# Half of a conformer's first pointwise product by seven products at the turn of groups, its weight sums kept in a buffer of x

## The chip, the cores and the metric

The kernel runs on one core of a Trainium2 chip. The metric is the device time of one launch in microseconds (us), the median of several runs. Of the five engines that run side by side, TensorE (PE) multiplies matrices into eight PSUM banks of 128 x 512 fp32; VectorE (DVE) and ScalarE (ACT) read these banks and work on SBUF; GpSimd (POOL) does small things; SyncE (SP) issues nearly all DMAs, in order. An engine runs its instructions in the order of the program and waits at semaphores.

## The reference, cut to what matters

A conformer block on x of 2 x 4000 x 512 in bf16: a feed-forward layer, attention over the 4000 tokens of a batch, a convolution module, a second feed-forward layer, with layer norms between. The change is about the start of the convolution module:

```
h = _layernorm(x2, axis=-1)
h = h @ w_pw1
a = h[..., :D].copy()
b = h[..., D:].copy()
h = a * _sigmoid(b)
```

D is 512, so w_pw1 has 512 rows and 1024 columns: "the first pointwise product". A depthwise convolution with three taps over the tokens follows.

## The kernel before, in words

Tokens go in 16 chunks of 512, 8 a batch; the last of each batch has 416 (`width`). Three stages follow each other: the first feed-forward layer over all chunks, the attention in 16 groups (one per chunk of queries, loop `attention`, L2050), and the second feed-forward layer. What is between attention and the second layer for chunk t (output projection, layer norm, pointwise product, gate, taps) is done beside the attention of the groups t + 1 and t + 2.

A group g runs through 32 steps kt. In the first group of a batch (g = 0 and 8, "plain") each step multiplies one tile of 128 keys with the queries (`scores`). In the others, steps 2 to 29 are taken four at a time by a quad (`score_quad`, L1993): a 2 x 2 block product of four key tiles is made from seven products instead of eight (Strassen's scheme in Winograd's form). Product k takes sums of key blocks times sums of query blocks; partial results are added in three PSUM banks (0, 1, 2, called c, x, h) and one SBUF buffer, m5. Its chain is: products 5 and 1, copied by ACT to m5 and h; product 6 added into h, then DVE writes x = h + m5; product 7 added into h, DVE writes m5 = h + m5; product 4 added into h. Products 2 and 3 go on top of c and x. ACT takes the exponentials. The values are multiplied in the same way (`pv`), products 2 and 4 of group g only in steps 2 to 6 of group g + 1 (`late_third`, L2133). The turn of groups, steps 30, 31, 0 and 1, has no quads.

The pointwise product (`pw1`, L2405) is made plainly before: for each of eight blocks of 128 channels four matmuls of 128 x 128 by 512 tokens, PSUM to `conv_b` (L2361: blocks of b, tanh of half of it by ACT) or `conv_a` (L2372: blocks of a, and the gate (tanh + 1) * a by DVE). `pair` (L2733) puts a block of b and one of a together and, two ticks on, the taps of the chunk before (`taps_beside`). Pairs 0 and 1 of chunk t stand at steps 24 and 28 of group t + 1, pairs 2 and 3 at steps 3 and 5 of group t + 2.

x of a chunk is fetched from DRAM for the residual (`get_x`, L2751, step 22) and stored again (`put_x`, L2754), in slots 0 and 1 of the buffer `xt` by turns during the attention. `touch` (L968) fills the unused 96 columns of bank 1 by a matmul for chunks of 416.

The order within each engine is not that of the program text. `Plan` (L110) collects all operations with modelled durations and simulates the engines; `choose` (L289) picks for PE, among the blocks ready within 8 us of modelled work behind the oldest open one, the one that can start first, and of equal ones the earlier in the text. All instructions are so emitted by L93.

Of the kernel before, what the change touches and what calls it, by code (L numbers as in the profile page):

```python
# [5 lines left out]
F32 = mybir.dt.float32  # L6
# [11 lines left out]
CHUNK = TPC * TILE  # L18
# [86 lines left out]
class Node:  # L105

    __slots__ = ("e", "emit", "dur", "land", "preds", "succs", "left", "ready", "late", "at", "seq", "ev", "size", "turn", "other")


class Plan:  # L110
# [7 lines left out]
    def __init__(self, sync, ahead, beside):  # L118
        self.S, self.ahead, self.beside = sync, ahead, beside
        self.nodes, self.pe, self.block = [], [], []  # L120
        self.w, self.r, self.d = {}, {}, {}
        self.table, self.same, self.first = None, [], None

    @staticmethod
# [48 lines left out]
    def new(self, e, dur, land, emit, reads, writes, dkeys=()):  # L173
        n = Node()
        n.e, n.dur, n.land, n.emit, n.preds, n.succs, n.seq, n.at = e, dur, land, emit, set(), [], len(self.nodes), len(self.pe)
        n.size, n.turn, n.other = 0, False, None
        self.nodes.append(n)
        n.preds |= self.link(n, reads, writes, dkeys)
        return n
# [92 lines left out]
    def once(self):  # L272
# [16 lines left out]
        def choose(e):  # L289
            if e == "PE":  # L290
                best = None
                for n in wait["PE"]:
                    k = index[n]
                    if T[k] - T[head] > self.beside:
                        continue
                    key = (max(free[e], n.ready - (40 if k == head else 0)), k)
                    if best is None or key < best[0]:
                        best = (key, n)
                return best and (max(free[e], best[1].ready), best[1])
            limit = T[head] + self.ahead  # L300
            found = [n for n in wait[e] if T[n.at] <= limit]
            if not found:
                return None
            now = max(free[e], min(n.ready for n in found))
            can = sorted([n for n in found if n.ready <= now], key=lambda n: (n.late, n.seq))
            soon = [n for n in found if n.ready > now]
            for n in can:
                end = now + max(n.other[e][0] if n.other else n.dur, n.size / 260) + self.OVER[e]
                if all(end <= u.ready + 60 or u.late >= end or u.late >= n.late for u in soon):
                    return now, n  # L310
            u = min(soon, key=lambda n: n.ready)
            return max(free[e], u.ready), u
# [37 lines left out]
class Sync:  # L350
# [125 lines left out]
    def emit_dma(self, engs, dkey, fns, reads, writes):  # L476
# [14 lines left out]
        self._bind(ev, reads, writes)  # L491
        return ev

    def planned(self, ahead, beside):
# [56 lines left out]
class Conformer:  # L551
# [35 lines left out]
    def memory(self):  # L587
# [114 lines left out]
        self.b_QF = [X.buf("QF", o, 4 * HC) for o in homes]  # L702
        self.m5s, self.b_m5s = X.view(18432 + 12 * HC, CHUNK, F32), X.buf("m5s", 18432 + 12 * HC, 4 * CHUNK)
        self.hv = A.view(TCB * 4096, 2 * PAIRS * D).rearrange("p (n k e d) -> p n k e d", k=2, e=2, d=HD)
        self.hq = A.view(2048, QUADS * 2048).rearrange("p (q u r e j k) -> p q u r e j k", q=QUADS, u=2, r=2, e=2, j=2)
# [152 lines left out]
        self.b_m3 = [C.buf("m3", oP + (self.NP - 1) * 1024 + j * 2 * TILE, 2 * TILE) for j in range(TPC)]  # L858

        self.last7, self.b_last7 = C.view(oLT + 4096, CHUNK), C.buf("last7", oLT + 4096, 2 * CHUNK)  # L860
        self.hl = C.view(oHL, 1024).rearrange("p (h c k) -> p h c k", h=2, c=DC)
# [102 lines left out]
    def mm(self, out, lhsT, rhs, start, stop, reads, bank, inc=None, **kw):  # L964
        self.S.op("PE", lambda e: e.matmul(out, lhsT, rhs, start=start, stop=stop, **kw),
                  reads=reads, writes=[bank], inc=stop if inc is None else inc)

    def touch(self, ps, b_ps, W):  # L968
        if W < CHUNK and b_ps is self.bank(1)[1]:
            x = self.hT[0][:, 0, 0, :]  # L970
            self.mm(ps[:, W:CHUNK], x, x[:, 0:CHUNK - W], False, True, [self.b_hT[0][0]], b_ps, skip_group_check=True)

# [664 lines left out]
    def q_group(self, b, qc, dc):  # L1637

        s, sl = qc % 2, self.query_slot(b, qc)
        ps, b_ps = self.sbank()  # L1640
        W = width(qc)
        lin, lo = self.queries(qc, sl)
        for cc in range(DC):
            self.mm(ps[:, 0:W], self.M[:, cc, dc * 128:(dc + 1) * 128], lin[:, cc, lo:lo + W],
                    cc == 0, cc == DC - 1, [self.b_M] + self.b_lnT[sl], b_ps)
        self.touch(ps, b_ps, W)
        self.act(self.qT[s][:, dc, 0:W], ps[:, 0:W], AF.Copy, [b_ps], [self.b_qT[s][dc]])
# [345 lines left out]
    def score_quad(self, g, q, step):  # L1993
# [34 lines left out]
        if step == 0:  # L2028
            product(5, h, b_h, True)
            self.act(m5, h[:, 0:W], AF.Copy, [b_h], [b_m5])  # L2030
            product(1, c, b_c, True)
# [18 lines left out]
    def attention(self, old, hook):  # L2050

        for g in range(NCK):
            W, plain = width(g), g % TCB == 0
            for kt in range(KT):
# [4 lines left out]
                if plain and kt < KT - 1 or kt < 2 or kt == KT - 2:  # L2059
                    ps, b_ps = self.scores(g, kt, None if plain else self.bank((0, 2)[kt] if kt < 2 else 0))  # L2060
                    if kt < KT - 2:
                        self.exp_pair(g, kt, ps, b_ps)
                    else:
                        self.act(self.P30[:, 0:W], ps[:, 0:W], AF.Exp, [b_ps], [self.b_P30], scale=SCALE)
                elif not plain and kt < KT - 2:
                    self.score_quad(g, *divmod(kt - 2, 4))
                if g == 0 and kt < 2:
                    self.pop(old // 2 if kt == 0 else old - old // 2)
# [8 lines left out]
                self.keys_swap(g, kt)  # L2077
                self.tick()

    @staticmethod  # L2080
# [324 lines left out]
    def pw1(self, t, cb, bank=None):  # L2405
# [9 lines left out]
        for out, x in moves:  # L2415
            for cc in range(DC):
                self.mm(out, self.Wp1[:, cc, cb * 128:(cb + 1) * 128], x[:, cc], cc == 0 and out is moves[0][0], cc == DC - 1,
                        [self.b_Wp1] + self.b_lnT[1 if t == NCK - 1 else 0], b_ps, skip_group_check=True)
        if t < NCK - 1:
            self.touch(ps, b_ps, W)  # L2420
        return ps, b_ps
# [46 lines left out]
    def fetch_conv(self, t):  # L2468
        W = width(t)
        self.load(self.dcv4[t][:, :, 0:W], self.dcvd[t].rearrange("p (c k) -> p c k", c=DC)[:, :, 0:W], self.b_dcv[t],  # L2470
                  reads=self.b_dcvd[t])

    def halo_left(self, t, jj):
# [155 lines left out]
    def program(self, any_score):  # L2629
# [100 lines left out]

        tail = NCK - 2

# [8 lines left out]
        def att_hook(g, kt):  # L2741
            if g == 0 and kt == 8:
                self.load(self.Wp1, i["w_pw1"].rearrange("(c p) f -> p c f", p=128), [self.b_Wp1])
            if kt in here and (0 <= g - 1 < tail or g - 1 == tail and here.index(kt) < self.KEEP):
                pair(g - 1, here.index(kt), self.bank(1) if kt == 24 else None)
            if 0 <= g - 2 < tail and kt in there:
                pair(g - 2, 2 + there.index(kt))
            if g == 0 and self.rest:
                self.load_rest(FC + kt, 3)
            if kt == (12 if any_score else 22):  # L2750
                self.get_x(g, self.slot(g, 0, 2))  # L2751
            if g and kt == 9 and not any_score:
# [14 lines left out]

        last = NCK - 1
        if any_score:
# [257 lines left out]
```

## Time and profile before

| | |
|---|---|
| median of three runs | 1884.49 us (1883.29 to 1886.34) |
| the profiled execution | 1882.47 us |
| its span, first to last instruction | 1878.7 us |
| DVE busy | 1463.0 us |
| ACT busy | 1306.9 us |
| TensorE clock granted | 1.0 of full speed |

In the profile a row gives line, engine, operation, what is written and read by the program's names (`s` are the banks 0 to 3, `y` the banks 4 to 7, `work`, `wff`, `keys`, `sums` and `xt` are SBUF regions), shapes, count, then busy us, mean ns of one, and the idle time before with its releaser. In the timeline a row is start, duration, engine, operation. PE's matmuls overlap, so that the duration of one holds the latency of its end.

### The profile page before, as it was taken

To read this page: it belongs to the slowest core of one execution; us is meant where nothing else is said; L and a number is where in the kernel's file an instruction comes from. 1 tells how busy PE (TensorE), PEld (TensorE's weight loads), DVE (VectorE), ACT (ScalarE), POOL (GpSimd) and SP (SyncE) were. 2 spreads that over 40 slices of the span, in tenths; PEclk is the share of its full clock that TensorE was granted. 3 is DMA by queue.
4 is the path that set the end of the run, shared out by engine and by line. 5 is a ranking of instruction groups with operands and counts; after the bars stand their busy time and mean duration, and the time that the engine had idled before them with its cause. 6 is when DMAs were issued, how large, how long until landed. Compare 5 with 4: busy or idle time off the path is not lost.

```text
span 1878.7 us, 39230 instructions
## 1 busy us (share of the span) xinstructions
PE 1860.1 (99%) x15389; PEld 1442.7 (77%) x15389; DVE 1463.0 (78%) x3191; ACT 1306.9 (70%) x2419; POOL 133.2 (7%) x301
## 2 busy tenths in 40 slices
PE   9999999999999999999999999999998999999998
PEld 5888888866777777777677777777774888888886
DVE  7888888868667777776777677768778888888885
ACT  5777777644667777677667677777668687777773
POOL 1000000000000000000000000000011000000000
PEclk9999999999999999999999999999999999999999
DMA  7323344197545555447944444444375222222111
GB/s 191 101 79 91 80 113 105 57 265 214 173 144 151 158 170 166 107 133 177 248 125 133 130 122 114 122 137 121 111 203 171 74 61 71 77 46 61 49 43 33
DMA packets 325014, 231.52 MB, mean 123 GB/s; under 512 B 204179, under 2 KB 295638, under 8 KB 324566
## 3 DMA queue, kind: packets, MB, share of 16 engines
q1 hardware_dynamic: 324294, 228.68, 44.4%
q8 instruction: 123, 2.02, 0.4%
q14 instruction: 69, 0.57, 0.1%
q10 hardware_dynamic: 528, 0.26, 0.0%
HBM read 128.44 MB, written 55.79 MB: 98 GB/s over the span
## 4 chain that ended last, share of the span: by engine, by line
PE 97%; DVE 1%; ACT 1%; DMA 0%; issue 0%; DVEq 0%; ACTq 0%
PE s L93 48%; PE y L93 48%; DVE work L93 1%; ACT work L93 0%; DMA xt<-v12d 0%; DVE wff L93 0%; DVE xt L93 0%; DVE s L93 0%; ACT sums L93 0%; DMA work<-work 0%; ACT wff L93 0%; ACT keys L93 0%; ACT s L93 0%; ACT xt L93 0%; ACT L93 0%
## 5 line engine op out<-in xcount | busy, mean ns | idle before, releaser
L93 ACT ACTIVATE sums<-s 128x512 bf16<-128x512 f32 (+2 forms) x494 | 288.2, 584 | 171.3 <-PE s L93 169.9
L93 ACT ACTIVATE keys<-s 128x512 bf16<-128x512 f32 (+2 forms) x284 | 165.6, 588 | 183.6 <-PE s L93 166.4
L93 DVE TENSOR_TENSOR sums<-sums 128x512 bf16<-128x512 bf16 (+3 forms) x528 | 195.4, 398 | 75.0 <-ACT sums L93 70.0
L93 PE MATMUL y<-work,keys 128*128 128x256 bf16 x1920 | 244.6, 273 | 0.0
L93 PE MATMUL s<-work,keys 128*128 128x256 bf16 (+5 forms) x1456 | 224.5, 292 | 0.0
L93 ACT ACTIVATE work<-xt,work 128x512 bf16<-128x512 bf16 x268 | 206.7, 785 | 7.8 <-DVE work L93 7.8
L93 PE MATMUL y<-wff,keys 128*128 128x256 bf16 (+3 forms) x1592 | 209.1, 276 | 0.1
L93 PEld LDWEIGHTS y<-work,keys 128*128 128x128 bf16 x1920 | 187.8, 98 | 25.1
L93 PE MATMUL y<-sums,keys 128*128 128x256 bf16 (+1 forms) x1440 | 202.6, 270 | 0.0
L93 PE MATMUL s<-sums 128*128 128x256 bf16 x1296 | 193.8, 273 | 0.0
L93 DVE TENSOR_TENSOR keys<-keys 128x1024 bf16<-128x1024 bf16 (+2 forms) x262 | 169.2, 662 | 28.8 <-ACT keys L93 13.6
L93 PE MATMUL y<-work,wff 128*128 128x256 bf16 (+2 forms) x1116 | 184.0, 292 | 0.0
L93 PEld LDWEIGHTS y<-wff,keys 128*128 128x128 bf16 (+1 forms) x1592 | 151.2, 98 | 32.4 <-issue 3.3
L93 DVE BATCH_NORM_STATS2 work<-xt 128x6 f32<-128x512 bf16 x251 | 163.9, 680 | 5.1 <-DMA xt<-in_x_dram 4.3
L93 PEld LDWEIGHTS s<-work,keys 128*128 128x128 bf16 (+1 forms) x1456 | 119.2, 97 | 50.6 <-ACT sums L93 4.0
L93 PEld LDWEIGHTS y<-sums,keys 128*128 128x128 bf16 x1440 | 138.8, 98 | 24.1 <-DVE sums L93 0.6
L93 POOL TENSOR_TENSOR work<-work 128x4 f32<-128x4 f32 (+3 forms) x107 | 89.8, 840 | 807.4 <-DVE work L93 804.9
L93 PE MATMUL s<-work,wff 128*128 128x512 bf16 (+5 forms) x668 | 141.0, 345 | 3.2 <-DVE work L93 2.7
L93 PEld LDWEIGHTS s<-sums 128*128 128x128 bf16 x1296 | 126.7, 98 | 20.0
L93 PE MATMUL s<-work 128*128 128x512 bf16 (+4 forms) x565 | 138.5, 375 | 3.0 <-DVE work L93 1.8
L93 PE MATMUL y<-sums,xt 128*128 128x256 bf16 (+1 forms) x960 | 139.4, 270 | 1.5 <-DVE sums L93 0.8
L93 PEld LDWEIGHTS y<-work,wff 128*128 128x128 bf16 x1116 | 108.2, 98 | 29.8
(143 smaller groups left out, 3202.2 us busy)
## 6 DMA issues: line engine op xcount, KB each, us to landing
xt<-kfd SPq DMA_DIRECT2D x98, 384.0 KB, 3.3
xt<-v12d SPq DMA_DIRECT2D x105, 256.0 KB, 2.9
xd<-xt SPq DMA_DIRECT2D x28, 512.0 KB, 3.1
xt<-xd SPq DMA_DIRECT2D x28, 512.0 KB, 4.3
out_dram<-xt SPq DMA_DIRECT2D x14, 512.0 KB, 3.0
xt<-in_x_dram SPq DMA_DIRECT2D x13, 512.0 KB, 4.0
dcvd<-wff SPq DMA_DIRECT2D x48, 128.0 KB, 2.1
keys<-dcvd SPq DMA_DIRECT2D x12, 512.0 KB, 4.3
```

The costliest lines, as they stand in the source:

```text
L93: return getattr(eng, self.name)(*self.args, **self.kw)
```

## The change

For chunks 0 to 6 and 8 to 13 (`by_unit`) pairs 0 and 1 are replaced by a unit of seven products (`gate_unit`) in four parts: at steps 30 and 31 of group t + 1 and 0 and 1 of group t + 2; where group t + 2 is plain, the last three all at step 31. It uses banks 0, 1, 2 and the m5 buffer of the quads. Its left blocks are channels of a and b (256 each) by halves of the 512 rows; its right ones are halves of the rows by halves of the tokens. Each product is four matmuls of 256 columns. The weights' sums (`gate_weights`) are made once, in group 0, into slot 1 of `xt`; the tokens' differences (`gate_tokens`) for each chunk at steps 26 to 29, into the buffer that the layer norm used. The pairs at steps 24 and 28 are then pairs 2 and 3. x of a chunk is fetched at step 26 and always into slot 0, of the last chunk into slot 1.

Besides: product 5 of a quad goes to bank x instead of h; the single scores of steps 0 and 1 both go to bank 0 (1 used bank 2 before); `touch` goes; and the planner's rule for equal blocks of PE compares modelled start times, in which the quads are put 1000 ns ahead (`front`).

```diff
@@ -120 +120 @@
+        self.front = 0
@@ -173 +174 @@
         n.e, n.dur, n.land, n.emit, n.preds, n.succs, n.seq, n.at = e, dur, land, emit, set(), [], len(self.nodes), len(self.pe)
-        n.size, n.turn, n.other = 0, False, None
+        n.size, n.turn, n.other, n.front = 0, False, None, self.front
@@ -293 +294 @@
-                    key = (max(free[e], n.ready - (40 if k == head else 0)), k)
+                    key = (max(free[e], n.ready - (40 if k == head else 0)), T[k] - n.front)
                     if best is None or key < best[0]:
@@ -491 +492 @@
+    def front(self, ns):
+        if self.plan:
+            self.plan.front = ns
     def planned(self, ahead, beside):
@@ -701 +706 @@
         self.m5s, self.b_m5s = X.view(18432 + 12 * HC, CHUNK, F32), X.buf("m5s", 18432 + 12 * HC, 4 * CHUNK)
+        self.WS = X.view(4096, 2048).rearrange("p (m j d) -> p m j d", m=4, j=2)
+        self.b_WS = [X.buf("WS", 4096 + m * 1024, 1024) for m in range(4)]
@@ -857 +864 @@
+        self.TF = [C.view(oLM + m * 1024, 512).rearrange("p (t j k) -> p t j k", t=2, j=2) for m in range(4)]
+        self.b_TF = [C.buf("TF", oLM + m * 1024, 1024) for m in range(4)]
+        self.th2 = W.view(24576, 2 * CHUNK, F32).rearrange("p (u k) -> p u k", u=2)
@@ -964 +974 @@
-    def touch(self, ps, b_ps, W):
-        if W < CHUNK and b_ps is self.bank(1)[1]:
-            x = self.hT[0][:, 0, 0, :]
-            self.mm(ps[:, W:CHUNK], x, x[:, 0:CHUNK - W], False, True, [self.b_hT[0][0]], b_ps, skip_group_check=True)
@@ -1643 +1648 @@
                     cc == 0, cc == DC - 1, [self.b_M] + self.b_lnT[sl], b_ps)
-        self.touch(ps, b_ps, W)
         self.act(self.qT[s][:, dc, 0:W], ps[:, 0:W], AF.Copy, [b_ps], [self.b_qT[s][dc]])
@@ -2026 +2030 @@
         if step == 0:
-            product(5, h, b_h, True)
-            self.act(m5, h[:, 0:W], AF.Copy, [b_h], [b_m5])
+            product(5, x, b_x, True)
+            self.act(m5, x[:, 0:W], AF.Copy, [b_x], [b_m5])
             product(1, c, b_c, True)
@@ -2049 +2053 @@
+        S = self.S
         for g in range(NCK):
@@ -2057 +2062 @@
                 if plain and kt < KT - 1 or kt < 2 or kt == KT - 2:
-                    ps, b_ps = self.scores(g, kt, None if plain else self.bank((0, 2)[kt] if kt < 2 else 0))
+                    ps, b_ps = self.scores(g, kt, None if plain else self.bank(0))
                     if kt < KT - 2:
...
                 elif not plain and kt < KT - 2:
+                    S.front(1000)
                     self.score_quad(g, *divmod(kt - 2, 4))
+                    S.front(0)
+                self.unit_steps(g, kt)
                 if g == 0 and kt < 2:
@@ -2076 +2084 @@
                 self.tick()
+    UNIT = (30, 31, 32, 33)
+    def unit_steps(self, g, kt):
+        if g == 0 and 24 <= kt < 28:
+            self.gate_weights(kt - 24)
+        for t, at in ((g - 1, kt), (g - 2, kt + KT)):
+            if self.by_unit(t):
+                if 26 <= at < 30:
+                    self.gate_tokens(at - 26)
+                for n, k in enumerate(self.UNIT):
+                    if min(k, KT - 1) == at if (t + 2) % TCB == 0 else k == at:
+                        self.gate_unit(t, n)
@@ -2416 +2438 @@
-        if t < NCK - 1:
-            self.touch(ps, b_ps, W)
         return ps, b_ps
@@ -2469 +2489 @@
+    @staticmethod
+    def by_unit(t):
+        return 0 <= t < NCK - 2 and t % TCB != TCB - 1
+    def gate_weights(self, step):
+        S = self.S
+        a11, a12, a21, a22 = [self.Wp1[:, 2 * e:2 * e + 2, lo:lo + 256] for lo in (D, 0) for e in range(2)]
+        s1, s2, s4, s3 = [self.WS[:, m] for m in range(4)]
+        b1, b2, b4, b3 = [[b] for b in self.b_WS]
+        out, x, y, op, rd, wr = ((s1, a21, a22, ALU.add, [], b1), (s2, s1, a11, ALU.subtract, b1, b2),
+                                 (s4, a12, s2, ALU.subtract, b2, b4), (s3, a11, a21, ALU.subtract, [], b3))[step]
+        S.op("DVE", lambda e: e.tensor_tensor(out=out, in0=x, in1=y, op=op), reads=rd + [self.b_Wp1], writes=wr)
+    def gate_tokens(self, step):
+        q = lambda e, k: self.lnT[0][:, 2 * k:2 * k + 2, 2 * e:2 * e + 2, :]
+        t1, t2, t4, t3 = self.TF
+        b1, b2, b4, b3 = [[b] for b in self.b_TF]
+        out, x, y, rd, wr = ((t1, q(0, 1), q(0, 0), [], b1), (t2, q(1, 1), t1, b1, b2), (t3, q(1, 1), q(0, 1), [], b3),
+                             (t4, q(1, 0), t2, b2, b4))[step]
+        self.S.op("DVE", lambda e: e.tensor_tensor(out=out, in0=x, in1=y, op=ALU.subtract),
+                  reads=rd + self.b_lnT[0], writes=wr)
+    def gate_unit(self, t, step):
+        S = self.S
+        (c, b_c), (x, b_x), (h, b_h) = [(ps[:, 0:CHUNK], b) for ps, b in (self.bank(k) for k in range(3))]
+        m5, b_m5 = self.m5s, self.b_m5s
+        raw = lambda e, lo: (lambda u, j: self.Wp1[:, 2 * e + j, lo + u * 128:lo + (u + 1) * 128], self.b_Wp1)
+        sums = lambda m: (lambda u, j: self.WS[:, m, j, u * 128:(u + 1) * 128], self.b_WS[m])
+        q = lambda e, k: (lambda j: self.lnT[0][:, 2 * k:2 * k + 2, 2 * e + j, :], self.b_lnT[0][2 * k:2 * k + 2])
+        form = lambda m: (lambda j: self.TF[m][:, :, j, :], [self.b_TF[m]])
+        forms = {1: (raw(0, D), q(0, 0)), 2: (raw(1, D), q(1, 0)), 3: (sums(2), q(1, 1)), 4: (raw(1, 0), form(2)),
+                 5: (sums(0), form(0)), 6: (sums(1), form(1)), 7: (sums(3), form(3))}
+        def product(k, ps, b_ps, start=False):
+            (a, b_a), (m, b_m) = forms[k]
+            for u in range(2):
+                out = ps[:, u * 256:(u + 1) * 256].rearrange("p (t k) -> p t k", t=2)
+                for j in range(2):
+                    self.mm(out, a(u, j), m(j), start and u == 0 and j == 0, u == 1 and j == 1,
+                            [b_a] + b_m, b_ps, skip_group_check=True)
+        def plus(out, b_out):
+            S.op("DVE", lambda e: e.tensor_tensor(out=out, in0=h, in1=m5, op=ALU.add), reads=[b_h, b_m5], writes=[b_out])
+        half = lambda k: self.th2[:, :, k * 256:(k + 1) * 256]
+        two = lambda ap: ap.rearrange("p (u k) -> p u k", u=2)
+        g = self.G[t % 2]
+        def tanh(src, b_src, k):
+            self.act(half(k), two(src), AF.Tanh, [b_src], self.b_th, scale=0.5)
+        def gate(src, b_src, k):
+            wr = [b for jj in range(2) for b in (self.b_G[t % 2][jj], self.b_Gl[t % 2][jj], self.b_Gr[t % 2][jj])]
+            S.op("DVE", lambda e: e.scalar_tensor_tensor(
+                out=g[:, 0:2, 1 + k * 256:1 + (k + 1) * 256], in0=half(k), scalar=1.0, in1=two(src), op0=ALU.add, op1=ALU.mult),
+                reads=[b_src] + self.b_th, writes=wr)
+        if step == 0:
+            product(5, x, b_x, True)
+            self.act(m5, x, AF.Copy, [b_x], [b_m5])
+            product(1, c, b_c, True)
+            self.act(h, c, AF.Copy, [b_c], [b_h])
+        elif step == 1:
+            product(6, h, b_h)
+            plus(x, b_x)
+            product(2, c, b_c)
+            tanh(c, b_c, 0)
+        elif step == 2:
+            product(7, h, b_h)
+            plus(m5, b_m5)
+            product(3, x, b_x)
+            tanh(x, b_x, 1)
+            gate(m5, b_m5, 1)
+        else:
+            product(4, h, b_h)
+            gate(h, b_h, 0)
+            for jj in range(2):
+                self.halo_left(t, jj)
+                self.halo_right(t, jj)
+                if t:
+                    self.after(2 + 2 * jj, lambda jj=jj: self.taps_beside(t - 1, jj))
@@ -2728 +2831 @@
-        tail = NCK - 2
+        tail, last = NCK - 2, NCK - 1
@@ -2742 +2845 @@
             if kt in here and (0 <= g - 1 < tail or g - 1 == tail and here.index(kt) < self.KEEP):
-                pair(g - 1, here.index(kt), self.bank(1) if kt == 24 else None)
-            if 0 <= g - 2 < tail and kt in there:
+                pair(g - 1, here.index(kt) + 2 * (not any_score and self.by_unit(g - 1)), self.bank(1) if kt == 24 else None)
+            if 0 <= g - 2 < tail and kt in there and (any_score or not self.by_unit(g - 2)):
                 pair(g - 2, 2 + there.index(kt))
...
                 self.load_rest(FC + kt, 3)
-            if kt == (12 if any_score else 22):
-                self.get_x(g, self.slot(g, 0, 2))
+            if kt == (12 if any_score else 26):
+                self.get_x(g, self.slot(g, 0, 2) if any_score else int(g == last))
             if g and kt == 9 and not any_score:
@@ -2765 +2868 @@
-        last = NCK - 1
```

2 lines of the change are left out of this document (1 added, 1 removed).

## The prediction

> **What bounds the kernel now.** I read the page's busy times and its chain first, then who TensorE (PE) waited for inside the attention, then PE's timeline at one turn of groups.
>
> ```profile
> span 1878.7 us, 39230 instructions
> ...
> PE 1860.1 (99%) x15389; PEld 1442.7 (77%) x15389; DVE 1463.0 (78%) x3191; ACT 1306.9 (70%) x2419; POOL 133.2 (7%) x301
> ...
> PE 97%; DVE 1%; ACT 1%; DMA 0%; issue 0%; DVEq 0%; ACTq 0%
> ```
>
> PE is busy for 99% of the span and is 97% of the chain that ended last. The profiled execution took 1882.47 us: its span and 3.8 us around it. It lies 2.0 us under the median of the three runs, 1884.49 us; I work out a difference on the trace and take it from that median.
>
> Busy time doesn't say what one matmul costs, since consecutive ones overlap. Their cost is the distance from one start to the next. The timeline at the turn from group 2 to group 3, with the third and fourth block pair of chunk 1 (the `work,wff` rows):
>
> ```profile
> 585.39 0.28 PE L93 MATMUL y<-wff,keys 32*128 32x256 bf16 x1
> ...
> 586.60 1.47 PE L93 MATMUL y<-sums,keys 128*128 128x256 bf16 x12
> 587.91 0.60 PE L93 MATMUL s<-xt 128*128 128x256 bf16 x4
> ...
> 590.09 1.89 PE L93 MATMUL y<-work,wff 128*128 128x512 bf16 x8
> 591.82 0.60 PE L93 MATMUL s<-xt,keys 128*128 128x256 bf16 x4
> ...
> 595.75 1.89 PE L93 MATMUL y<-work,wff 128*128 128x512 bf16 x8
> ...
> 648.66 0.28 PE L93 MATMUL y<-wff,keys 32*128 32x256 bf16 x1
> ```
>
> Twelve matmuls of 256 columns take 587.91 - 586.60 = 1.31 us, 0.109 us each. Eight of 512 take 591.82 - 590.09 = 1.73 us, 0.216 us each. The two `wff,keys` rows are the same place of two successive groups: a group takes 63.27 us. Its work, counted from the code: 414 narrow matmuls (196 of scores, 210 and 8 of values) are 45.1 us, 76 wide ones (12 scores, 16 queries, 16 output, 32 of the first pointwise product) 16.4 us, the few matmuls on strips of 32 rows or columns some 0.7 us. That is 62.2 of 63.27 us. So PE is packed in the attention, and what one takes out of its work comes off the time unless a new hole opens. Reordering alone can win at most about 1 us in a group. The holes that the trace names, from 480 to 1420 us:
>
> ```profile
> PE s L93 <- DVE s L93: 2.3, 6, 0.4
> PE s L93 <- DVE xt L93: 1.5, 3, 0.6
> PE s L93 <- DVE work L93: 1.0, 1, 1.0
> PE y L93 <- DVE sums L93: 0.8, 2, 0.4
> PE y L93 <- DMA xt<-v12d: 0.6, 1, 0.6
> PE y L93 <- ACT keys L93: 0.2, 1, 0.2
> ```
>
> Fourteen waits, 6.4 us. The first two rows, 3.8 us, are the score quads: a product waiting for VectorE (DVE) to add m5 into a bank, or to have read it.
>
> **What the change takes out of PE.** For 13 of the 16 chunks (0 to 6 and 8 to 13) two of the four block pairs go: 4 blocks of 4 wide matmuls, 16 x 0.216 = 3.46 us. In their place stand seven products of 4 narrow ones, 28 x 0.109 = 3.05 us. A chunk saves 0.41 us; unrounded (1.73/8 and 1.31/12) it is 0.403, and 13 of them 5.2 us.
>
> The Trainium skill ("TensorE: Matmul & The Clock Gate", Back-to-back issue gap) gives two prices: 512/2.4 + 2.5 ns for an isolated gap, and about 131 ns for 512 and 81 ns for 128 columns as the sustained roofline of weight load and matmul pairs. By the second, with an estimate of 98 ns for 256 columns between its two figures, the change would cost 28 x 98 - 16 x 131 = 0.65 us more in a chunk. This kernel is a stream of such pairs and shows 0.216 us, so the trace disagrees with the second price and fits the first.
>
> The five filler matmuls of `touch` go as well:
>
> ```profile
> L93 PE MATMUL s<-keys 128*128 128x96 bf16 x5 | 1.0, 204 | 0.0
> ```
>
> At the narrow rate 96 columns are 0.04 us each, 0.2 us in all; the row's busy time, 1.0 us, is the upper bound. I take 0.2.
>
> **What it adds beside PE.** Prices from groups of the same shape between 526 and 1400 us:
>
> ```profile
> L93 DVE TENSOR_TENSOR s<-s,xt 128x512 f32<-128x512 f32 x77 | 53.7, 697 | 31.8 <-PE s L93 24.8 <-ACT work L93 6.6
> L93 DVE TENSOR_TENSOR xt<-s,xt 128x512 f32<-128x512 f32 x77 | 53.0, 688 | 38.4 <-PE s L93 38.2
> ...
> L93 DVE SCALAR_TENSOR_TENSOR wff<-wff,s 128x512 bf16<-128x512 f32 x27 | 18.5, 686 | 1.7 <-PE s L93 0.9 <-ACT wff L93 0.3
> ...
> L93 DVE TENSOR_TENSOR xt<-work,xt 128x512 bf16<-128x512 bf16 x20 | 8.4, 419 | 2.2 <-PE s L93 2.2
> ...
> L93 ACT ACTIVATE xt<-s 128x512 f32<-128x512 f32 x76 | 45.4, 598 | 52.5 <-PE s L93 51.9
> L93 ACT ACTIVATE s<-s 128x512 f32<-128x512 f32 x76 | 44.2, 582 | 5.9 <-PE s L93 3.8
> ```
>
> DVE gets four differences of tokens for a chunk (4 x 0.42 = 1.7 us) and two additions (0.69 each, 1.4 us): 3.1 us in a group of 63.3. Its two gates at 0.69 stay two, and the taps stay as many; they change places. ScalarE (ACT) gets two copies, 1.2 us, its tanh stay two. The four sums of weights come once, 1.7 us of DVE in group 0. None of this is on PE's path by amount. By place it could be:
>
> ```profile
> 576.00:579.00 3.00, 3.00 (x26) 2.15 (x24) 2.49 (x7) 2.85 (x6) 0.00 (x0) 1.00 0.33 72
> 579.00:582.00 3.00, 3.00 (x20) 1.72 (x19) 3.00 (x10) 2.63 (x5) 0.26 (x1) 1.00 0.44 154
> 582.00:585.00 3.00, 3.00 (x23) 2.09 (x22) 3.00 (x8) 1.80 (x5) 1.11 (x2) 1.00 0.21 61
> 585.00:588.00 3.00, 3.00 (x32) 2.33 (x30) 3.00 (x8) 2.73 (x6) 0.00 (x0) 1.00 0.43 136
> 588.00:591.00 3.00, 3.00 (x26) 2.30 (x25) 2.97 (x8) 0.70 (x2) 0.00 (x0) 1.00 0.34 69
> 591.00:594.00 3.00, 3.00 (x25) 2.31 (x24) 1.70 (x4) 2.66 (x10) 0.31 (x2) 1.00 0.51 167
> 594.00:597.00 3.00, 3.00 (x24) 2.15 (x22) 1.75 (x5) 3.00 (x7) 0.00 (x0) 1.00 0.90 182
> 597.00:600.00 3.00, 3.00 (x26) 2.29 (x25) 1.99 (x4) 2.43 (x5) 0.30 (x2) 1.00 1.08 243
> ```
>
> The columns after the stretch and its length are busy time of PE, weight load, DVE, ACT, POOL. DVE has no gap from 579 to 591 us, just at the turn where the unit is put, and only 1.3 + 1.25 + 1.0 = 3.6 us of gaps in the 9 us behind it. The unit's additions and gates (2.8 us) must fall there; the token differences (1.7 us) can be done before, since the chunk's transposed tokens are there before its first block pair. So DVE is nearly full for 20 us around each of 13 turns. The unit is a chain: five products in a row each wait for the reader before (0.44 us of matmuls and some 0.16 us until the last is out: of 587.91's four 0.60 us, less 0.44), with two copies, two additions and a gate between, 3.0 + 0.60 + 0.58 + 0.70 + 0.69 + 0.69 = 6.3 us. It is spread over four steps of 63.27 / 32 = 1.98 us, 7.9 us. What hides it is late value work that PE may take early: 60 narrow matmuls (6.5 us) of products 2 and 4, and the planner lets PE reach 8 us ahead. But 1.73 us x 2 of wide matmuls that fed PE right behind the turn (590.09 and 595.75) are gone. If the cover fails, the whole excess is PE's.
>
> The cost of this is not in the trace. Its bounds: from nothing (a unit that fits, as the quads do with 14 short waits in 900 us) to 2.8 us a turn, 36 us in all (the full DVE time that falls into the gapless stretch). The nearer row is the wait list: of 98 score quads, with the same chain and length, nine waits are on record, 3.8 us, 0.04 us a quad. A turn is tighter than a quad, so I take twice that, 0.08 us, 1.0 us for 13.
>
> **Order and queues.** Product 5 of a quad goes to the second bank and no longer waits for the last exponential of the quad before, and quads stand 1000 ns ahead in PE's order where two are ready. Both aim at the 3.8 us of score waits, with about 0.16 us of pipeline refilling each that the busy time hides, 9 x 0.16 = 1.4: 5.2 us at most. Against them stands that values then come later. Bounds: 5.2 gained to the same lost; I take 1.5 us gained, under a third.
>
> x of a chunk now has one home, not two. Its load must wait until the store of the chunk before has read it:
>
> ```profile
> 611.81 0.43 SPq L93 DMA_DIRECT2D xt<-xd  x1
> ...
> 614.75 0.32 SPq L93 DMA_DIRECT2D xd<-xt  x1
> ```
>
> ```profile
> xd<-xt SPq DMA_DIRECT2D x28, 512.0 KB, 3.1
> ```
>
> The load went 2.9 us ahead of the store; it must now stand behind it, and behind its landing (3.1 us by the page's median for these). x is first used at step 9 of the next group, some 50 us later, so this costs nothing by itself. On SP's in-order queue the streams of keys and values stand behind it. Their price when late is the one `v12d` wait, 0.6 us; I take nothing, and keep 0.6 in each of 14 groups, 8 us, as the other end.
>
> **Sum.** -5.2 - 0.2 + 1.0 - 1.5 = -5.9 us: 1876.6 on the profiled execution, **1878.6 us** beside the median.
>
> **The rivals.**
>
> *The holes close too.* If the score waits go and the turn adds none, the sum is -5.2 - 0.2 - 5.2 = -10.6, but of the 3.8 us these four rows, all in the two groups of 416 queries, hold 1.6:
>
> ```profile
> 875.52 0.53 PE L93 MATMUL s<-xt,keys 128*128 128x208 bf16 x4 [0.41 <-DVE s L93]
> ...
> 881.39 0.53 PE L93 MATMUL s<-xt,keys 128*128 128x208 bf16 x4 [0.41 <-DVE s L93]
> ...
> 1374.17 0.53 PE L93 MATMUL s<-xt,keys 128*128 128x208 bf16 x4 [0.41 <-DVE s L93]
> ...
> 1380.02 0.53 PE L93 MATMUL s<-xt,keys 128*128 128x208 bf16 x4 [0.41 <-DVE s L93]
> ```
>
> There narrow products are 208 columns, PE has less to fill with, and the wait may only move. So half is likelier: -8, 1876.5. In its favour: the freed bank; against: DVE, which released them, gets more work. In full it gives 1873.9.
>
> *The turn takes it back.* A hole of 0.41 us at each turn eats the whole saving: 1884. For it speaks the gapless DVE; against it the 8 us that PE may reach ahead.
>
> *Slower: DVE's queue at the turn.* The gates and additions stand in DVE's queue ahead of the next group's first additions into its score banks and of the joins that free the value banks. Beyond the point where 2.8 us of extra DVE work exceeds the late value work that is ready, PE stops for the rest. At 1.2 us a turn, under half the extra, 13 turns cost 15.6: 1884.5 - 5.4 + 15.6 = 1895. It decides from 0.7 us a turn, where the time is 0.2% up.
>
> *Narrow matmuls cost more than half of wide ones.* They would have to cost over 3.46 / 28 = 0.124 us; rows of 12 and 4 show 0.109. Chance under 0.01. That fewer products are replaced than said I also give nothing: 13 follows from the conditions in the code.
>
> **Chances.** 0.2% of the time, 3.8 us, is about what a measurement here tells from none. Forecast (1876.5 to 1880.7): 0.48. Holes close (under 1876.5): 0.22. Both are faster: 0.70. The turn takes it back (1880.7 to 1888.3): 0.17. Slower: 0.13. The range of 8 in 10 goes from 1873.0 to 1886.0: some 0.04 lies below, 0.15 above.
>
> **What would show it.** In the changed trace narrow matmuls from `work,wff` into `s` banks are up by 13 x 28 = 364 (some with sums as operands), wide ones down by 208, and a group in the middle is about 62.8 us long. If it is as long as before, the PE waits at the turns have grown, with DVE as releaser. Waits on `s` for DVE should be below 3.8 us if the bank and the order do what I think. A `v12d` or `kfd` wait in many groups would show the SP queue. The forecast is wrong if the turn's holes exceed 0.4 us each, or if the new order of the whole plan moves the feed-forward stages, which I take as unchanged.

## The result, and the profile after

The changed kernel takes 1888.32 us (median of 18 runs, 1884.96 to 1890.29), the kernel before 1883.32 us beside it (18 runs): 5.0 us more, a ratio of 1.0025 with a 95% interval of 1.0018 to 1.0032. The forecast was 5.9 us less. The profiled execution took 1888.21 us. The head of its page:

```profile
span 1884.3 us, 39474 instructions
...
PE 1851.9 (98%) x15417; PEld 1457.0 (77%) x15540; DVE 1490.8 (79%) x3267; ACT 1320.8 (70%) x2451; POOL 137.1 (7%) x301
...
PE 55%; ACT 3%; DVE 2%; DMA 1%; issue 1%; POOL 0%; DVEq 0%; SPq 0%; ACTq 0%
```

The matmuls are there as worked out: 15540 weight loads, which are the 15389 of before, less 208 wide and 5 fillers, and 364 narrow more (123 matmul records of this trace are missing, so its PE count and busy time are a little low). By that count PE has 5.4 us less to do, and the span is 5.6 us longer: some 11 us have been lost elsewhere. The named waits hold 6.4 us of it, and two stretches at half clock another 3.4 us by the granted clock (last section). Whom PE waited for from 400 to 1420 us, total, times and longest, all but the waits of 0.2 us:

```profile
PE s L93 <- ACT s L93: 3.4, 6, 1.1
PE s L93 <- DVE s L93: 2.9, 1, 2.9
PE s L93 <- DVE sums L93: 2.5, 5, 1.3
PE y L93 <- DVE sums L93: 1.5, 2, 1.2
PE s L93 <- ACT sums L93: 1.5, 5, 0.4
PE s L93 <- DVE work L93: 1.0, 1, 1.0
```

12.8 us in 20 waits against the 6.4 us of before, and of other kinds: the short waits of quads for DVE's additions are gone (one long one of 2.9 us is left), and PE waits for sums of values (`sums`) and for ACT's copy of c into h (`s`). What DVE and ACT themselves wait for tells why. The groups of VectorE by form (busy, mean ns | idle before, releaser) have one that was not there before:

```profile
L93 DVE TENSOR_TENSOR work<-work 128x512 bf16<-128x512 bf16 x52 | 21.2, 420 | 21.4 <-DMA work<-work 21.2
```

These are the token differences, 13 x 4. DVE stands idle for 21.2 us in front of them until a DMA lands: the transposes that bring the chunk's tokens in order (`ln_beside`). The timeline of DVE and then of PE at steps 20 to 21 of group 2:

```profile
562.75 0.69 DVE L93 TENSOR_TENSOR xt<-s,xt 128x512 f32<-128x512 f32 x1 [0.83 <-PE s L93]
566.24 0.88 DVE L93 TENSOR_TENSOR work<-work 128x512 bf16<-128x512 bf16 x2 [2.79 <-DMA work<-work]
567.04 1.33 DVE L93 TENSOR_TENSOR sums<-sums 128x512 bf16<-128x512 bf16 x3
```

```profile
566.65 0.60 PE L93 MATMUL s<-work,keys 128*128 128x256 bf16 x4
567.60 0.60 PE L93 MATMUL y<-sums,xt 128*128 128x256 bf16 x4 [0.35 <-DVE sums L93]
568.43 0.61 PE L93 MATMUL s<-sums,keys 128*128 128x256 bf16 x4 [0.23 <-DVE sums L93]
```

The three value sums stand in DVE's queue behind two token differences that the planner had moved ahead from steps 26 and 27, and these wait 2.79 us for their tokens. How long the sums themselves were held up, the run with the differences held shows below: about 1.5 us, since their last exponential was not done before 565.6 us. PE then runs out of values. At the turn to the plain group 8 the same wait, 3.09 us, makes the one long hole of PE (2.88 us): an addition of a quad stands behind it. This turn alone is dear. From 842.50 to 964.95 us, the starts of groups 7 and 9, it is 122.45 us, and 118.13 us where both waits are gone (the run "both held").

A second queue does the like. Right behind the turn ACT adds up the row sums of the group before, which a DMA has transposed:

```profile
592.83 0.71 ACT L93 ACTIVATE wff<-wff,work 128x512 bf16<-128x512 bf16 x1
595.50 0.42 ACT L93 ACTIVATE work<-work 128x256 bf16<-128x256 bf16 x1 [1.96 <-DMA work<-work]
...
599.68 0.59 ACT L93 ACTIVATE s<-s 128x512 f32<-128x512 f32 x1
```

```profile
598.02 1.25 PE L93 MATMUL y<-sums,work 128*128 128x256 bf16 x10
600.33 0.61 PE L93 MATMUL s<-xt 128*128 128x256 bf16 x4 [1.05 <-ACT s L93]
```

ACT waits 1.96 us for the DMA, its exponentials and copies come late, and product 6 of a quad (the `s<-xt` row) waits 1.05 us for the copy of c into h. ACT had this wait before too, and more of it, 16.0 us in 10 groups against 6.6 us in 6 here, with no wait of PE for ACT's copies on record there.

### The profile page after: what moved, and what is told of

The parts are those of the page before. It is cut to its first block, busy times and chain, and to the rows that moved or that the text cites. A ratio compares the mean times of both kernels' runs of the same rounds, so it can differ in the third digit from the quotient of the medians.

```text
span 1884.3 us, 39474 instructions
## 1 busy us (share of the span) xinstructions
PE 1851.9 (98%) x15417; PEld 1457.0 (77%) x15540; DVE 1490.8 (79%) x3267; ACT 1320.8 (70%) x2451; POOL 137.1 (7%) x301
## 4 chain that ended last, share of the span: by engine, by line
PE 55%; ACT 3%; DVE 2%; DMA 1%; issue 1%; POOL 0%; DVEq 0%; SPq 0%; ACTq 0%
PE s L93 29%; PE y L93 26%; DMA work<-work 1%; DVE work L93 1%; ACT work L93 1%; ACT sums L93 1%; DVE sums L93 0%; ACT wff L93 0%; DVE xt L93 0%; DVE wff L93 0%; ACT xt L93 0%; ACT s L93 0%; ACT keys L93 0%; DVE keys L93 0%; DVE s L93 0%
## 5 line engine op out<-in xcount | busy, mean ns | idle before, releaser
L93 PE MATMUL s<-work,keys 128*128 128x256 bf16 (+4 forms) x1420 | 217.3, 289 | 2.7 <-ACT sums L93 0.7
L93 PE MATMUL y<-sums,keys 128*128 128x256 bf16 (+1 forms) x1440 | 214.0, 270 | 0.0
L93 PE MATMUL y<-wff,keys 128*128 128x256 bf16 (+2 forms) x1590 | 208.7, 276 | 0.4 <-DVE xt L93 0.4
L93 PE MATMUL s<-work,wff 128*128 128x512 bf16 (+5 forms) x808 | 162.1, 333 | 3.1 <-DVE work L93 2.1
L93 PE MATMUL y<-sums,xt 128*128 128x256 bf16 (+1 forms) x960 | 147.6, 270 | 1.5 <-DVE sums L93 1.5
L93 PE MATMUL y<-work,wff 128*128 128x256 bf16 (+1 forms) x924 | 139.3, 273 | 0.2 <-ACT keys L93 0.2
L93 PE MATMUL s<-work 128*128 128x512 bf16 (+4 forms) x513 | 124.3, 375 | 6.0 <-DVE work L93 1.8
L93 PE MATMUL s<-xt,keys 128*128 128x256 bf16 (+1 forms) x816 | 124.6, 271 | 2.9 <-DVE s L93 2.9
```

Of the source, the lines that this page charges most:

```text
L93: return getattr(eng, self.name)(*self.args, **self.kw)
```

## The experiments

Theory A: token differences at the head of DVE's in-order queue, ahead of the landing of their tokens, hold up value sums. Rivals: B, DVE and ACT have too much to do at the turn (the prediction's slower rival); C, the precedence of the quads starves PE later. D, the same kind of wait at the head of ACT's queue, and E, too long a chain for the work left at the turn, came with the second set. Each run was timed in five rounds beside the kernel before; the differences below are to its median in the same set (1883.77, 1883.67 and 1884.09 us; in the first row 1883.32 us).

| run | us | to the kernel before | ratio, 95% interval |
|---|---|---|---|
| the change | 1888.32 | +5.0 | 1.0018 to 1.0032 |
| differences held | 1879.40 | -4.4 | 0.9965 to 0.9986 |
| no precedence | 1883.45 | -0.3 | 0.9993 to 1.0011 |
| small parts alone | 1878.25 | -5.5 | 0.9957 to 0.9981 |
| no differences | 1877.97 | -5.8 | 0.9963 to 0.9983 |
| both held | 1873.49 | -10.2 | 0.9933 to 0.9961 |
| differences held, pairs behind | 1875.07 | -8.6 | 0.9940 to 0.9968 |
| bank alone | 1879.69 | -4.0 | 0.9966 to 0.9984 |
| precedence alone | 1882.56 | -1.1 | 0.9986 to 1.0004 |
| row sums held | 1877.35 | -6.7 | 0.9950 to 0.9977 |
| small parts, row sums held | 1876.62 | -7.5 | 0.9948 to 0.9975 |
| both held, no precedence | 1875.29 | -8.8 | 0.9938 to 0.9965 |
| both held, pairs behind | 1870.67 | -13.4 | 0.9918 to 0.9945 |

**Differences held.** The planner takes an operation up to 16 us of modelled work ahead of its place. A field takes this back for the differences:

```diff
-            found = [n for n in wait[e] if T[n.at] <= limit]
+            found = [n for n in wait[e] if T[n.at] + n.hold <= limit]
...
+                    self.S.hold(16000)
                     self.gate_tokens(at - 26)
+                    self.S.hold(0)
```

> The changed kernel, but the planner may not move the token differences ahead of their place in the program (steps 26 to 29); nothing else is touched. Theory A (a token difference stands at the head of VectorE's queue before its transposed tokens have landed, 10 waits of 21.2 us in the changed kernel's trace, and what is queued behind it comes late for TensorE): these waits go, the TensorE waits on sums and on s with VectorE as releaser at steps 22 to 26 go with them (some 8 us with the slow clock after the longest), and the time falls to about 1880 us, below the kernel before. Theory B (VectorE and ScalarE have too much to do at the turn itself): the differences then fall into the turn, and the time stays at 1888 us or rises to 1892 us. Theory C (the quads put ahead starve TensorE later): no change, 1888 us.

1879.40 us: 9 us gone, below the kernel before. The row of the token differences in this trace:

```profile
L93 DVE TENSOR_TENSOR work<-work 128x512 bf16<-128x512 bf16 x52 | 21.6, 418 | 0.0
```

As much work, no wait, and no wait of PE for `sums` from DVE is left. A holds. B, that the differences are then in the way at the turn, doesn't. The three value sums of the timeline above, in this trace:

```profile
564.32 1.34 DVE L93 TENSOR_TENSOR sums<-sums 128x512 bf16<-128x512 bf16 x3 [2.17 <-ACT sums L93]
```

This group starts 1.22 us earlier than in the change (524.87 and 526.09 us), so on the clock of the change they start at 565.5 us instead of 567.04. PE still waits for ACT, the first line of its waits:

```profile
PE s L93 <- ACT s L93: 4.1, 6, 1.7
```

**No precedence.** `S.front(1000)` to `S.front(0)`.

> The changed kernel with the quads no longer put 1000 ns ahead. Theory C (the precedence of the quads makes values late): 1882 to 1884 us. Theories A and B: within 2 us of the changed kernel, 1886 to 1890 us, and VectorE still waits some 20 us for the transposed tokens.

1883.45 us, where C stood; but DVE's wait for the tokens fell too, from 21.2 to 8.2 us in 7 groups, against what A expected. Every edit makes the planner order everything anew, and this order happened to have fewer differences too early. What waits were left still cost PE: it waits 8.0 us in 8 waits for DVE's additions, and seven of these end 1 to 2.4 us behind a wait of DVE for tokens (2.77 us of DVE up to 878.47 us, then 2.55 us of PE up to 879.96). So A's waits are there without the precedence too; here additions of quads stand behind the differences. The time doesn't part A from C; the next run and "both held, no precedence" do.

**Small parts alone.** No units; bank x for product 5, single scores in bank 0, precedence, no fillers:

```diff
-        return 0 <= t < NCK - 2 and t % TCB != TCB - 1
+        return False
```

and the sums of weights and the move of `get_x` taken back.

> The kernel before with the small parts of the change alone: product 5 of a quad in bank x, the single scores in bank 0, quads 1000 ns ahead, no filler matmuls. No units and no weight sums; x has its two homes. As the prediction had it: 1.5 to 5 us below the kernel before, 1878 to 1882 us. Theory C: 2 to 5 us above it, 1885 to 1888 us. Theories A and B: nothing of the loss is here, 1880 to 1884 us.

1878.25 us, 5.5 less than before. C falls for a kernel without units: the precedence costs nothing there. The units cost 10 us on top in the change as it is.

**No differences.**

```diff
-                 5: (sums(0), form(0)), 6: (sums(1), form(1)), 7: (sums(3), form(3))}
+                 5: (sums(0), q(0, 0)), 6: (sums(1), q(0, 1)), 7: (sums(3), q(1, 0))}
...
-                if 26 <= at < 30:
-                    self.gate_tokens(at - 26)
```

and product 4 likewise.

> The changed kernel without the four token differences of each chunk: products 4 to 7 read the tokens themselves, so the gate is computed from other numbers; the matmuls and all else stay. It takes away the wait for the transposed tokens and 1.7 us of VectorE work in each group. Theory A: as with the differences held back, about 1879 to 1880 us. Theory B: half of VectorE's extra work goes, 1884 to 1886 us. If this one is well below the one that holds them back, the amount of work counts, and not the wait alone.

1877.97 us. Taking the work away as well gives 1.4 us more than taking the wait away, with intervals that overlap. So it is the wait; what the work itself costs can't be told from nothing.

**Both held.** The row sums of ACT in addition:

```diff
+                S.hold(16000)
                 self.act(x, x, AF.Copy, self.b_sT, [self.b_sqs[s][ti]], accum_out=self.sq[s][:, ti:ti + 1])
+                S.hold(0)
```

> The first run's kernel (token differences held back) with one more set of operations held at its place in the program: the four sums of the row sums on ScalarE at step 7, which read tokens transposed by DMA. In the first run's trace ScalarE waits 7.0 us for these DMAs in 6 groups, and TensorE 4.1 us for ScalarE's copies of c into h in the same groups. Theory D (the same trap a second time, on ScalarE's queue, now that the wide matmuls behind the turn are gone): both waits go, and the time falls by 3 to 5 us from 1879.4 us, to 1875 us; the units then give most of the 5 us that their matmuls save. Theory E (the chain of unit and first quad is itself too long for what TensorE has to do at the turn): within 1.5 us of 1879.4 us.

1873.49 us, 5.9 less than with the differences alone: D. ACT has no wait for these DMAs any more:

```profile
L93 ACT ACTIVATE work<-work 128x256 bf16<-128x256 bf16 x56 | 22.4, 404 | 0.0
```

Where D's wait sat with the differences held shows best in groups 10 to 13. ACT and then PE of that run, at the turn to group 11:

```profile
1094.39 0.42 ACT L93 ACTIVATE work<-work 128x256 bf16<-128x256 bf16 x1 [2.41 <-DMA work<-work]
```

```profile
1096.32 0.61 PE L93 MATMUL s<-xt 128*128 128x256 bf16 x4 [1.75 <-ACT s L93]
```

PE has four such waits there, 3.2 us. The four groups take 254.6 us with the differences held and 250.7 us with both held. The start of two groups of the new run, by the same matmul as in the prediction:

```profile
587.45 0.28 PE L93 MATMUL y<-wff,keys 32*128 32x256 bf16 x1
...
650.09 0.28 PE L93 MATMUL y<-wff,keys 32*128 32x256 bf16 x1
```

62.64 us. With the small parts alone it was 63.11 us, in its trace:

```profile
584.77 0.28 PE L93 MATMUL y<-wff,keys 32*128 32x256 bf16 x1
...
647.88 0.28 PE L93 MATMUL y<-wff,keys 32*128 32x256 bf16 x1
```

That is 0.47 us; over the eight ordinary groups 2 to 5 and 10 to 13 it is 0.45 us each (505.1 us against 501.5). The 0.40 us that a unit's matmuls were to save in a group are there once the holes are not.

**Differences held, pairs behind.** Pairs 2 and 3 back at steps 3 and 5 behind the turn, nothing at 24 and 28. In this kernel the taps of two blocks get into each other's buffers, so the convolution is computed from other numbers; the operations are the same.

```diff
-            if 0 <= g - 2 < tail and kt in there and (any_score or not self.by_unit(g - 2)):
+            if 0 <= g - 2 < tail and kt in there:
```

> The first run's kernel with pairs 2 and 3 of a chunk left at steps 3 and 5 of the next group, as before, and nothing at steps 24 and 28: the wide matmuls behind the turn are back. Theory E, and the prediction's word on the cover that is gone: the waits of TensorE on ScalarE's copy behind the turn go, and the time falls by 2 to 4 us from 1879.4 us, if no hole opens at steps 24 to 28. Theory D: a smaller gain, under 2 us, since ScalarE's queue still waits for the DMA.

1875.07 us, 4.3 below the run with the differences held, though ACT still waits 6.5 us for its DMAs, in 6 groups. ACT waits 1.08 us up to 523.08 us, for instance, with no wait of PE behind it, and PE's waits for ACT's copies fall from 4.1 to 1.2 us. The wide matmuls behind the turn cover most of that wait: this is E's number, and it says that the wait became a hole because the cover was gone. Whether the cover is whole it doesn't say; see the last run.

**Bank alone** and **precedence alone**, each on the kernel before:

```diff
-            product(5, h, b_h, True)
-            self.act(m5, h[:, 0:W], AF.Copy, [b_h], [b_m5])
+            product(5, x, b_x, True)
+            self.act(m5, x[:, 0:W], AF.Copy, [b_x], [b_m5])
```

> The kernel before with one edit: product 5 of a quad in bank x. It may start before the last exponential of the quad before. If the 5.5 us of the third run come from the bank: 1878 to 1880 us. If from the precedence: 1882 to 1884 us.

> The kernel before with one edit: the quads 1000 ns ahead in TensorE's order. If the 5.5 us of the third run come from the precedence: 1878 to 1880 us. If from the bank: 1882 to 1886 us. If both are needed, neither this nor the one before is under 1881 us.

1879.69 and 1882.56 us: 4.0 us from the bank, 1.1 from the precedence, which alone can't be told from nothing. Added up they are 5.1 of the 5.5.

**Row sums held**, the differences left free.

> The changed kernel with only the row sums on ScalarE held at step 7; the token differences stay free to go ahead. It parts the loss between the two queues. If the two waits cost about what the runs before say one after the other (9 us for VectorE's, 6 us for ScalarE's): 1882 to 1884 us. If VectorE's wait alone makes the loss and ScalarE's only shows once it is gone: 1887 to 1889 us.

1877.35 us, under both expectations: each of the two sets, held alone, gives back 9 to 12 us of a loss that is 15 us in all. They don't add since the new plan also had DVE's wait down from 10 to 5 groups, 9.3 us. In the first groups, where the plan is still nearly the same, they part. The distances from the start of one group to that of the next, by the first `wff,keys` rows of each as above:

| groups | before | change | differences held | row sums held | both held |
|---|---|---|---|---|---|
| 2 to 3 (DVE waits at 566 us) | 63.09 | 63.74 | 62.66 | 63.79 | 62.66 |
| 3 to 4 (ACT waits at 595 us) | 63.27 | 63.82 | 63.58 | 62.60 | 62.64 |

Of the change and of the run with the row sums held, the first of these stretches:

```profile
526.09 0.28 PE L93 MATMUL y<-wff,keys 32*128 32x256 bf16 x1
...
589.83 0.28 PE L93 MATMUL y<-wff,keys 32*128 32x256 bf16 x1
...
653.65 0.28 PE L93 MATMUL y<-wff,keys 32*128 32x256 bf16 x1
```

```profile
526.04 0.28 PE L93 MATMUL y<-wff,keys 32*128 32x256 bf16 x1
...
589.83 0.28 PE L93 MATMUL y<-wff,keys 32*128 32x256 bf16 x1
...
652.43 0.28 PE L93 MATMUL y<-wff,keys 32*128 32x256 bf16 x1
```

The group with DVE's wait gets 1.1 us shorter by holding the differences and none by holding the row sums. So does the one before it (DVE waits 1.63 us up to 503.97 us): 1.4 us and none. The next one, with ACT's wait, gets 1.2 us shorter by holding the row sums. Its 63.58 us with the differences held say nothing against this: ACT has no such wait there in that run, and PE's 0.52 us for ACT's copy at 628 us come of exponentials that stand behind four operations of the layer norm in ACT's queue (`work<-xt,work`, 2.92 us).

**Small parts, row sums held.**

> The third run's kernel (small parts alone, no units) with the row sums on ScalarE held at step 7. In its trace ScalarE waits 15.8 us for these DMAs in 11 groups. If that wait is covered there, by the wide matmuls of pairs 2 and 3 behind the turn: no gain, 1877 to 1879 us. If the wait costs by itself, whatever stands behind the turn: 3 to 6 us less, 1872 to 1875 us, and the units then give nothing on top.

1876.62 us: 2.0 us better against its kernel before than without (-7.5 and -5.5), with intervals that overlap, and just under the first expectation, though 15.8 us of waits went. Without units that wait is mostly covered; with them it cost 5.8 us (differences held and both held).

**Both held, no precedence.**

> Both sets held (the run of 1873.5 us) and the quads not put 1000 ns ahead. If the precedence is worth what it was in the kernel before, 1.1 us: 1874 to 1875.5 us. If it is worth what it was with the bank, or in the changed kernel, more: 1876 to 1879 us; if it costs, under 1873 us.

1875.29 us, -8.8 against -10.2: the precedence is worth about what it was alone, and again not told from nothing. No cost of it shows with units either, once no queue waits, so C falls here too.

**Both held, pairs behind**, the edits of both those runs, and the taps of pairs 2 and 3 one tick later, so that the buffers hold:

```diff
-                self.after(3, lambda: self.taps_beside(t - 1, jj))
+                self.after(4 if self.by_unit(t) else 3, lambda: self.taps_beside(t - 1, jj))
```

> Both sets held, and pairs 2 and 3 left at steps 3 and 5 of the next group, their taps one tick later. The candidate to beat all. If each of the two (no waiting queue, wide matmuls behind the turn) removes the same holes: 1872 to 1874 us, no more than the run of 1873.5 us. If they remove different ones: 1869 to 1871 us.

1870.67 us, the fastest: 13.4 us below the kernel before, ratio 0.9931 (0.9918 to 0.9945). It is 3.2 us better than both held by the differences, with intervals that overlap. What the pairs behind the turn did here is not shown: PE's named waits are as long in both traces (3.9 us from 420 to 1405 us), and so are groups 2 to 6 (312.5 and 312.3 us) and 10 to 13. The 3.2 us between the two traces lie in the first and last groups of each batch (2.0) and in the second feed-forward stage (1.2). Against the differences held with pairs behind it is 4.8 us better; the held row sums or the later taps make this, which was not parted, so whether the cover was whole there stays open. Its units now give what their matmuls promise: 5.9 us on top of the small parts with the row sums held (-13.4 and -7.5; each of the two is known to some 2.5 us either way).

## Why the prediction was wrong, step by step

**The products, -5.2 us.** Right. 0.45 us for an ordinary group, and 5.9 us for all between two runs in which next to no queue waits. **The fillers, -0.2 us**, were not tried apart; they are in the 5.5 us of the small parts.

**The order, -1.5 us.** Right in sign, too small: 5.5 us with the fillers, at the bound of 5.2 and the 0.2 of these. Nearly all is the bank (4.0); "I take 1.5 us gained, under a third" is the term, and it was one of choice. That the bound was met is in part luck, for the gain is not where the score waits were looked for. The eight ordinary groups together are 505.1 us with the small parts alone and 505.6 before; of 7.0 us less in the attention of the two traces, 6.5 lie in the groups at both ends of a batch. Why the bank helps there stays open.

**The turn, +1.0 us.** This step failed. It read: "the token differences (1.7 us) can be done before, since the chunk's transposed tokens are there before its first block pair". They are there before the block pair, at step 24 (in group 2 they land by 566.24 us and the pair starts at 570.36), but the planner may go 16 us ahead, and it put differences in DVE's queue in front of where the DMA lands. The step counted how much DVE gets to do and never asked what the new operations wait for, nor who stands behind them in an in-order queue. In its place the runs showed operations waiting for DMAs at the head of DVE's queue, and of ACT's once the cover was gone. From the change to both held this is 1888.32 to 1873.49 us, 15.2 us by the differences to the kernel before, in place of 1.0. Up to 2 us of it are not the units' doing, since holding the row sums gave that without them. The 15.2 us also hold the stretch at half clock behind the longest hole. The step's own bounds, nothing to 36 us, hold the 15.2; the choice of 1.0 rested on the quads' waits for additions, which is another wait.

**The cover behind the turn.** "1.73 us x 2 of wide matmuls that fed PE right behind the turn [...] are gone" was named as the risk and is shown where ACT's queue waits: with pairs 2 and 3 back there the time is 4.2 us lower by the differences with the row sums free. With them held it is 3.2 us lower, but there the traces show no hole at an ordinary turn that it closed. I had priced it by quads, 0.08 us a turn.

**The rivals.** The slower one had the sign and DVE's queue, by the wrong mechanism: not more work than PE can bridge at the turn, but waits for DMAs in two queues, one of them some eight steps ahead of the turn. That quads come first costs nothing by itself; in the change as it is, taking it away gave 4.9 us, with DVE's waits for tokens down from 21.2 to 8.2 us. The store and load of x in one home, for which I kept 8 us, shows in no wait of PE for a load of keys or values.

**The feed-forward stages**, taken as unchanged, hold part of the loss: from the first `wff,keys` row of the last group to the end it is 1884.3 - 1394.92 = 489.4 us against 1878.7 - 1391.71 = 487.0. With both held and the pairs behind it is 1866.1 - 1379.23 = 486.9. The units are not needed for this: the small parts alone take 489.8 us there. Both traces have a stretch at half clock in it, shown below, which is worth 1.7 us by the granted clock. Six of the fourteen traces have one in this stage, two of them of kernels without units, and the kernel before has none. The rest was not tried apart.

## What to carry to other kernels

An operation added to a queue that runs in order is priced by what it waits for and by what stands behind it, before its own length: look up where its inputs land, and how far ahead a planner may put it. When work moves away from a place, find whose waits it had been covering there; they needn't have changed to become holes. And where a planner orders everything anew, compare the stretches in which the plan is still the same before adding up whole times.

## What the runs showed of the hardware

Behind a hole of 3.0 us in PE its granted clock fell to half for a while. The hole goes from 881.0 us, when the eight matmuls of the first row below have been issued at 0.09 us each, to 884.0; by its record it is 2.88 us. In the changed kernel PE's timeline and the windows of 2 us (PE, weight load, DVE, ACT, POOL, then the granted clock):

```profile
880.27 0.88 PE L93 MATMUL y<-sums,xt 128*128 128x208 bf16 x8
884.02 0.88 PE L93 MATMUL s<-xt,keys 128*128 128x208 bf16 x4 [2.88 <-DVE s L93]
...
885.38 1.91 PE L93 MATMUL s<-work,wff 128*128 128x512 bf16 x4
887.23 0.37 PE L93 MATMUL s<-work,keys 128*32 128x104 bf16 x16
```

```profile
882.00:884.00 2.00, 0.00 (x0) 0.00 (x0) 1.47 (x4) 0.00 (x0) 0.00 (x0) 0.95 1.10 319
884.00:886.00 2.00, 1.98 (x10) 1.49 (x11) 1.53 (x4) 0.37 (x1) 0.00 (x0) 0.50 0.94 195
886.00:888.00 2.00, 2.00 (x26) 0.84 (x24) 1.04 (x3) 1.25 (x4) 0.00 (x0) 0.70 0.34 79
```

Four wide matmuls take 887.23 - 885.38 = 1.85 us, some twice the 0.87 us of four at 0.216. By the granted clock some 1.6 us of PE's work is lost on top of the hole (half of 2 us and 0.3 of the next 2). The Trainium skill ("TensorE: Matmul & The Clock Gate", What's actually happening) puts the fall to half clock after an idle window of about 3.4 us. The half agrees with the 0.50 measured here; a hole of 3.0 us was enough. One of 2.55 us by its record at the same turn, in the run without precedence, left the clock at 1.00. In the second feed-forward stage the same happens from 1436 us, behind several shorter holes:

```profile
1434.00:1436.00 2.00, 0.98 (x12) 0.72 (x9) 2.00 (x6) 1.91 (x5) 0.62 (x1) 1.00 1.10 341
1436.00:1438.00 2.00, 1.13 (x11) 0.66 (x8) 1.03 (x4) 1.39 (x3) 0.00 (x0) 0.69 1.08 391
1438.00:1440.00 2.00, 1.83 (x9) 1.35 (x10) 1.85 (x4) 1.90 (x4) 0.00 (x0) 0.50 1.02 399
1440.00:1442.00 2.00, 2.00 (x11) 0.83 (x10) 2.00 (x3) 1.53 (x3) 0.00 (x0) 0.96 0.29 117
```

The kernel before has holes of about the same size at this place (1.25, 0.24, 1.02, 0.35 and 0.61 us, here 1.25, 0.23, 1.02, 0.35 and 0.69), and its clock stays at 1.00. What decides is not shown. Both stretches come to the same: what the three windows lack of full clock is 0.85 x 2 us = 1.7 us, at half clock 3.4 us.
